# Batch 0 scores a tile whole in one step, tables first; all instruction orders set anew

## Chip, cores and metric

One NeuronCore of a Trainium2 chip runs one launch. The metric is device time in microseconds (us) of that core; times below are medians of whole launches, and the profile is one execution of the program.

## The reference, cut to what matters

Three layers run one after the other, in float32, on two batches (b = 0, 1) of 768 tokens and 512 channels (8 heads of 64).

```python
# 1. attention with a hash mask
q_bits = q @ proj > 0; k_bits = k @ proj > 0            # 6 bits each: a bucket of 64
scores = where(q_bucket == k_bucket, q @ k.T / 8, -1e9)
attn = exp(scores - max(scores)); attn /= sum(attn) + 1e-9
x = attn @ v                                            # heads side by side: 2 x 768 x 512
# 2. Fourier mixing and an MLP
u = x + real(fft2(x)); un = layernorm(u)
x = u + relu(un @ w_ch1) @ w_ch2                        # 512 -> 2048 -> 512
# 3. token mixing
theta = x @ w_theta
y = w_tok_r @ (x * cos(theta)) + w_tok_i @ (x * sin(theta))
u = x + y; out = u + relu(u @ w_ch)
```

The mask is computed as a product: a query has a one-hot vector of its bucket times a huge number, a key has its one-hot vector, and the product of the two is added to the scores in the same PSUM accumulator, so that a wrong bucket lies far below the maximum.

## The kernel before

All three layers are one program of 13,493 instructions on five engines, built in the order of a priority clock: `at(us)` sets the priority of what follows, `sooner(..)` moves it, and the table `T` holds some 300 such numbers. Batch 0's attention is different: `loop_ops` lists its steps with costs and buffers, `plan` orders them, and `attention_first` emits them in exactly that order (`Ordered.keep`). Priorities set an order when the program is built; on the chip each engine runs its own queue in that order and waits on semaphores.

The work in order of time:

- **Attention of batch 0**: four pairs of heads (`j`), per pair 12 tiles of 128 queries, head by head in turn; 48 tiles. Steps of a tile `n`: `S` (scores into a PSUM tile `pss` of two halves of 384 keys, a ring of three), `MAX` (VectorE), `EXP` (ScalarE), then either kind `d`: `HI` and `LO` split the weights into two float16 parts, `TR` transposes them by DMA; or kind `p`: `T` transposes on TensorE, `C` and `U` split. `AV` (18 small products) gives the output in `pso`, `N` normalises half a pair, `F` folds for the Fourier step.
- **How a score tile is made** (`phase_S`): a score half is a float32 product over the 64 dimensions of one head plus a bfloat16 product over 64 one-hot rows. Both use 64 of the 128 rows of TensorE, and the two row halves belong to the two heads. A step `S(n)` therefore does keys 384 to 767 of tile `n-1` and keys 0 to 383 of tile `n` (the other head) side by side, and `MAX(n)` needs `S(n+1)`.
- **Bits and patterns of a pair**: `load_pair` loads q and k transposed, `scale_pair` (GpSimd) scales k by 1/8, `bits_pair` does four products with `projb` and one comparison (`BP`, `BV`), `pattern_pair` does the one-hot vectors in four products with `pat` over 64 rows each (`PP`, `PA`).
- **Batch 1's attention** (`attention`, `prep`): scores there are float32r over stacks `stk` of 128 rows (high part, copy, low part, one-hot), four products a tile. `prep` loads (`tt`, `vr`), scales, makes bits, splits q and k and writes the one-hot rows. It runs beside the Fourier step of batch 0 (`Fft`, tables `ct`, `sn`, `dt` loaded on GpSimd's queue), the layer norm (`ln_first`, `layernorm`) and the MLP of batch 0 (`mlp1`, `mlp2`), whose weights are converted from an 8-byte form in pieces (`conv16`, `from_f64`: DMA `r`, two steps on ScalarE, one on VectorE, then a high and a low part).
- **Then** the Fourier step and MLP of batch 1, `theta`, `tok_sum` and `tok_out` of both batches, all on TensorE in dense order.

Products on data that nobody reads (`heat` before the first data, `fill` where batch 1 begins, 70 of them in `prep` and around the first tiles) fill stretches in which TensorE would have nothing to do. All of batch 0's instructions share line L64 and all others L62, since one helper records them; groups are told apart by tile names. Some tiles are borrowed: in batch 0 the names `w1h`, `w1l`, `p`, `pt` and `x` also stand for softmax tiles.

## Time and profile before

| | us |
|---|---|
| median of 3 launches | 710.55 (709.36 to 711.47) |
| the profiled execution | 712.29 |
| its span, first to last instruction | 710.5 |
| TensorE (PE) busy in the span | 663.8 (93%) |
| VectorE (DVE) | 415.6 (58%) |
| ScalarE (ACT) | 381.5 (54%) |
| GpSimd (POOL) | 313.7 (44%) |
| mean granted TensorE clock | 0.978 of full speed |

The profiled execution is 1.74 us above the median of the runs; 1.8 us of it lie outside the span. A busy share is a mean over stages with different limits: the stretches of time matter more than the totals here. SPq is the queue of SyncE, from which most DMAs start.

### The profile page before, as it was taken

The page shows a single profiled execution, that of the slowest core. Times are in us where ns is not written, and L with a number is a line of the kernel's source. Part 1 is how long each engine was busy: PE and PEld are TensorE (multiplying, and loading weights), DVE is VectorE, ACT ScalarE, POOL GpSimd, SP SyncE. Part 2 cuts the span into 40 slices and gives each one's busy share as a digit, 9 for nine tenths or more (in the row PEclk, how much of TensorE's full clock was granted, in tenths as well). Part 3 has the DMA queues.
Part 4 walks back from the last instruction along what each step waited for, and adds up shares of the span by engine and source line. Part 5 has one row for each costly group of instructions (what it writes and reads, how often), then busy time and mean ns, then how long its engine had stood idle before and what let it go on. Part 6 is the DMA issues. An engine that isn't in the chain of part 4 may idle for free.

```text
span 710.5 us, 13493 instructions
## 1 busy us (share of the span) xinstructions
PE 663.8 (93%) x5451; PEld 506.0 (71%) x5451; DVE 415.6 (58%) x687; ACT 381.5 (54%) x602; POOL 313.7 (44%) x257
## 2 busy tenths in 40 slices
PE   7899996896888889999999999999999999999998
PEld 2456664774675556866877687576685789999997
DVE  3668798869897568644494775452122676342222
ACT  4657887688788788463322176432026766720000
POOL 4678786576776566565020113421013457530000
PEclk9999999798899999999999999999999999999999
DMA  9987895596899997887450152100005723620202
GB/s 332 275 182 137 156 183 115 169 251 168 206 247 238 234 217 186 153 135 134 90 193 1 40 149 59 30 1 1 1 1 174 228 81 99 183 89 0 89 1 90
DMA packets 163038, 94.48 MB, mean 133 GB/s; under 512 B 138656, under 2 KB 149152, under 8 KB 162976
## 3 DMA queue, kind: packets, MB, share of 16 engines
q1 hardware_dynamic: 161040, 86.66, 52.1%
q0 software_dynamic: 1936, 6.96, 2.9%
q8 instruction: 43, 0.70, 0.4%
q14 instruction: 19, 0.16, 0.1%
HBM read 50.21 MB, written 6.29 MB: 80 GB/s over the span
## 4 chain that ended last, share of the span: by engine, by line
PE 26%; issue 11%; DMA 4%; POOL 3%; ACT 3%; DVE 3%; POOLq 0%; ACTq 0%; DVEq 0%; SPq 0%
PE psm L62 18%; PE psf L62 8%; DMA r<-in_wtok 3%; ACT r L62 1%; POOL w1l L62 1%; DMA x<-p 1%; POOL nn L62 1%; DVE u L62 1%; POOL wchl L62 1%; DMA r<-in_wch 1%; DVE rr L62 1%; ACT nn L62 0%; DVE xt L62 0%; POOL wthl L62 0%; ACT u L62 0%
## 5 line engine op out<-in xcount | busy, mean ns | idle before, releaser
L62 PE MATMUL psm<-unT,w1h 128*128 128x256 f16 x768 | 132.2, 276 | 2.5 <-DVE u L62 1.5
L62 PE MATMUL psm<-unT,w1l 128*128 128x256 f16 x384 | 106.0, 276 | 0.0
L62 PEld LDWEIGHTS <-w1h 128*128 128x128 f16 x768 | 75.3, 99 | 15.8 <-issue 3.4
L62 DVE SCALAR_TENSOR_TENSOR r<-r 128x512 uint32<-128x512 uint32 (+1 forms) x64 | 49.7, 779 | 52.5 <-ACT r L62 46.4
L62 PE MATMUL psm<-w2h,hl 128*128 128x512 f16 x192 | 73.2, 382 | 0.0
L62 PE MATMUL psm<-w2l,hh 128*128 128x512 f16 x192 | 72.9, 382 | 0.0
L62 PE MATMUL psm<-w2h,hh 128*128 128x512 f16 x192 | 72.3, 379 | 0.1
L62 POOL TENSOR_TENSOR w1l<-r,w1h 128x384 fp32r<-128x384 f32 (+1 forms) x33 | 36.9, 1129 | 76.6 <-ACT w1h L62 76.5
L62 ACT ACTIVATE r<-r,chalf 128x512 uint32<-128x512 uint32 (+1 forms) x64 | 46.0, 719 | 39.8 <-DMA r<-in_w 17.6
L62 PEld LDWEIGHTS <-hh 128*128 128x128 f16 x384 | 37.0, 98 | 42.5 <-issue 3.2
L62 ACT ACTIVATE hh<-psm 128x512 f16<-128x512 f32 x48 | 28.3, 592 | 65.7 <-PE psm L62 65.6
L62 DVE TENSOR_REDUCE nm<-pss 128x1 f32<-128x768 f32 x48 | 45.1, 949 | 21.0 <-PE pss L62 21.0
L64 PE MATMUL pss<-stk 64*128 64x384 f32 (+1 forms) x264 | 55.0, 482 | 0.8 <-ACT p L64 0.5
L64 DVE TENSOR_REDUCE nm<-pss 128x1 f32<-128x768 f32 x48 | 45.5, 954 | 16.1 <-PE pss L64 13.6
L62 DVE SCALAR_TENSOR_TENSOR hl<-psm,hh 128x512 f16<-128x512 f32 x48 | 32.9, 688 | 35.8 <-ACT hh L62 35.5
L62 PE MATMUL pss<-stk 128*128 128x384 f32 x192 | 47.9, 374 | 5.3 <-ACT p L62 4.7
L62 ACT ACTIVATE p<-pss,nm 128x768 f32<-128x768 f32 x43 | 38.4, 896 | 20.3 <-DVE nm L62 19.0
L62 POOL TENSOR_TENSOR p<-p,p 128x768 f16<-128x768 f32 x24 | 41.3, 1722 | 16.3 <-ACT p L62 10.6
L62 PEld LDWEIGHTS <-w1l 128*128 128x128 f16 x384 | 38.1, 99 | 6.0 <-issue 1.1
L62 PEld LDWEIGHTS pss<-stk 128*128 128x128 f32 x192 | 33.9, 199 | 10.2 <-ACT p L62 6.6
L62 ACT ACTIVATE r<-r 128x512 f32<-128x512 f32 (+1 forms) x64 | 39.4, 616 | 0.0
L62 PEld LDWEIGHTS <-hl 128*128 128x128 f16 x192 | 18.9, 98 | 21.2 <-issue 0.9
(333 smaller groups left out, 1572.2 us busy)
## 6 DMA issues: line engine op xcount, KB each, us to landing
r<-in_w SPq DMA_DIRECT2D x32, 512.0 KB, 4.7
r<-in_wtok SPq DMA_DIRECT2D x24, 384.0 KB, 3.6
vr<-in_v SPq DMA_DIRECT2D x8, 390.0 KB, 5.0
stk<-stk SPq DMA_DIRECT2D x16, 192.0 KB, 3.3
xT<-xs SPq DMA_DIRECT2D x12, 256.0 KB, 2.7
xt<-xT SPq DMA_DIRECT2D x4, 768.0 KB, 5.2
ct<-in_ct POOLq DMA_DIRECT2D x4, 579.0 KB, 7.2
sn<-in_sn POOLq DMA_DIRECT2D x4, 576.0 KB, 9.1
```

Source lines behind the costliest of these rows:

```text
L62: return fn(*a, **k)
L64: self.last = fn(*a, **k)
```

## The change

The table `T` is set anew throughout: costs (`du`), keys (`lk`), the kinds of the 48 tiles (`kq`, still 32 `d` and 16 `p`), engines (`hq`, and new `lq`, `pk`) and nearly all offsets. Two switches in it: `sf='rrrr'` leaves all four pairs of batch 1 in the form they had (float32r stacks of 128 rows; the new branch `whole` in `prep` is built for none), and `mt=0` lets `mlp2` run two token tiles in turns, in two PSUM tiles at once. In code:

```diff
-    projb = mk(const, [128, 32], F32, "projb")
+    small = mk(at_p, [128, 290], F32, "small")
+    proj, hb = small[:, 0:96].rearrange("p (a n) -> p a n", a=3), small[:, 96:98]
+    pats = mk(at_p, [128, 6, 128], BF16, "pats")
...
     def load_pair(j, n):
+            made[j] = [t[:, 0:2], two3(t[:, 2]), two3(t[:, 3].bitcast(BF16)), hk]
+        if n < 2:
+            SY.dma_start(out=made[j][0][:, n], in_=A["qd"][0, j, :, n])
+        else:
+            SY.dma_start(out=made[j][1] if j else raw, in_=A["kd"][0, j])
...
+    def bit_products(ps, q, k, h):
+        for g in range(2):
+            mm(ps[64 * h + 32 * g:64 * h + 32 * g + 32], proj[:, 0], q[:, h, 384 * g:384 * g + 384], True, g == 1)
+        mm(ps[64 * h:64 * h + 32], proj[:, 1], k[:, h], False, True)
...
     def pattern_pair(j, n, ps, by="v"):
+        if j:
+            mm(ps, pats[:, 3 * h + p], bits[j], True, True)
+        else:
+            mm(ps, pat[half[h], p], bits[j][half[h]], True, True)
...
-    def phase_S(n, ps):
-        for g, m in ((1, n - 1), (0, n)):
+    def halves_S(ps, ops, c, part=(0, 1)):
+        for k in part:
+            for g in range(2):
+                mm(ps[:, g, 0:384], ops[2 * k][half[g], c], ops[2 * k + 1][half[g]], k == 0, k == 1)
...
-            op(("MAX", n), "DVE", 0.87, n + 1, [("S", n + 1)])
+            op(("MAX", n), "DVE", 0.87, n + 1, [("S", n)])
-                op(("LO", n), "POOL", 1.7, n + 4, [("HI", n)], "", [("p", ("EXP", n))])
+                op(("LO", n), *(("DVE", 0.97) if T["lq"][n] == "v" else ("POOL", T["dl"])), n + 4, [("HI", n)], "", [("p", ("EXP", n))])
...
+                pt[n], turned = transposed(p2.pop(n))
+                for g, k in (("d1", 0), ("dw", 1)):
+                    if n >= T["cn"][k] and g not in gate:
+                        gate[g] = turned
...
-        with sooner("cl"):
+        with sooner("cl"), after_gate("dw"):
...
+            with after_gate("d1"):
+                ld.dma_start(out=o, in_=i[b, j])
```

In the diff, `small` holds `proj`, `hb` and the pattern tables in one load; `qd` is q of one head on both row halves, `kd` has keys 0 to 383 on the lower and 384 to 767 on the upper half; `T` has `cn=[31, 27]`. The two gates mean that the loads of batch 1's first q and k (`tt`) and of the first MLP weights (`r`) are issued only behind the transposes of batch 0's tiles from 31 and 27 on; nothing held them before. Counts by engine: five `LO` steps go from GpSimd to VectorE, two `HI` steps from ScalarE to GpSimd; a pair has six products for its bits (was four) and six for its patterns (was four), the results of the latter read by ScalarE (18) and VectorE (6), where it was ScalarE 13 times and VectorE once; three low parts of weights go from GpSimd and one high part from ScalarE to VectorE. The matrix products of the scores, `AV` and of all later layers are the same in number and shape. Runs of score products in batch 0 that stand between other work are 37, where 43 were.

The order as built, at three places. First SyncE's queue at the start (names `in_..` are inputs in HBM: `qT`, `kT`, `qd`, `kd` queries and keys, `w` MLP weights). Before:

```order
L64 DMA stk<-in_qT 128x768
L64 DMA stk<-in_kT 128x768
L62 DMA tt<-in_qT 128x768
L62 DMA tt<-in_kT 128x768
L62 DMA r_1895<-in_w 128x1024
L62 DMA r_1902<-in_w 128x1024
L62 DMA r_1909<-in_w 128x1024
L64 DMA vr<-in_v 128x780
L64 DMA stk<-in_qT 128x768
L64 DMA_TRANSPOSE w1h<-p_112 128x12x128 x2
```

and now:

```order
L64 DMA ident<-in_ident 128x128
L64 DMA pats<-in_pats 128x768
L64 DMA pat<-in_patr 128x256
L64 DMA stk<-in_qd 128x768 x2
L64 DMA stk<-in_kd 128x768
L64 DMA_TRANSPOSE pt<-p_112 128x12x128
L64 DMA vr<-in_v 128x780
L64 DMA_TRANSPOSE w1h<-p_112 128x12x128
```

The five loads of `tt` and `r` no longer stand ahead of the first transposes.

Second, TensorE at its first data (`zero` and, before, `w1h` are operands of `heat`; `x`, `w1l` are borrowed tiles of one-hot keys and raw keys). Before:

```order
L64 MATMUL pss<-stk,projb 32x384 x4
L64 LDWEIGHTS w1h
L64 MATMUL psm<-w1h 128x512
L64 LDWEIGHTS w1h
L64 MATMUL psm<-w1h 128x512
L64 LDWEIGHTS pat
L64 MATMUL pss<-bits,pat 128x384
```

and now:

```order
L64 MATMUL pso<-stk,small 32x384 x2
L64 MATMUL pso<-w1l,small 32x384
L64 MATMUL pss<-stk 128x384 x2
L64 LDWEIGHTS small
L64 MATMUL psm<-bits,small 128x384
L64 LDWEIGHTS small
L64 MATMUL pss<-bits,small 128x384
L64 MATMUL pso<-stk,small 32x384 x2
L64 MATMUL pso<-w1l,small 32x384
L64 LDWEIGHTS stk
L64 MATMUL pss<-x,stk 128x384
```

The first head's bits come alone, its first scores stand between bits and patterns, and the two `heat` products behind the bits are gone.

Third, VectorE where batch 0 ends and batch 1 begins (`psm<-pso,r` is the last normalisation, which frees `pso`; `vv<-vr,vv` is the low part of batch 1's values). Before:

```order
L62 TENSOR_SCALAR bits<-pss 64x768
L62 SCALAR_TENSOR_TENSOR stk<-tt,stk 64x768
L64 TENSOR_SCALAR r<-pso 128x6
L62 SCALAR_TENSOR_TENSOR vv<-vr,vv 128x780
L64 RECIPROCAL r<-r 128x6
L64 TENSOR_TENSOR psm<-pso,r 128x384
L62 TENSOR_TENSOR fa<-x,psm 128x6x64 x2
```

and now:

```order
L62 TENSOR_SCALAR bits<-pss 64x768
L62 SCALAR_TENSOR_TENSOR stk<-tt,stk 64x768
L64 TENSOR_TENSOR hlz_194<-zraw,hlz_194 128x6x64
L64 TENSOR_SCALAR r<-pso 128x6
L64 RECIPROCAL r<-r 128x6
L64 TENSOR_TENSOR psm<-pso,r 128x384
L62 SCALAR_TENSOR_TENSOR vv<-vr,vv 128x780
```

The values' step now follows the normalisation. On TensorE at this place 70 `fill` products stood ahead of batch 1's first two score tiles; now 50 stand ahead of the first tile and 20 more ahead of the next two. The first product of the batch 0 MLP stood behind 59 score tiles (11 of batch 1) and 54 `AV` steps, and stands behind 61 and 54.

## Rows read from the trace of the kernel before

**Rows 1.** The page: busy tenths in 40 equal slices, TensorE and its granted clock.

```profile
PE   7899996896888889999999999999999999999998
...
PEclk9999999798899999999999999999999999999999
```

**Rows 2.** Stretches: length, busy us (instructions) by engine, clock, DMA share, GB/s.

```profile
core 0: us, PE busy (x) PEld busy (x) DVE busy (x) ACT busy (x) POOL busy (x), PEclk, DMA share, GB/s
9.00:37.00 28.00, 23.81 (x181) 12.97 (x181) 18.22 (x21) 18.83 (x27) 18.50 (x19) 0.94 1.11 313
...
77.00:118.00 41.00, 40.27 (x594) 27.30 (x592) 35.19 (x57) 32.66 (x50) 30.43 (x22) 1.00 0.88 151
118.00:136.00 18.00, 9.58 (x98) 8.55 (x95) 16.64 (x26) 15.96 (x24) 9.27 (x6) 0.81 0.43 111
...
160.00:190.00 30.00, 20.47 (x154) 15.93 (x151) 27.77 (x59) 24.63 (x37) 19.65 (x15) 0.78 0.80 206
190.00:240.00 50.00, 45.52 (x464) 33.28 (x462) 39.50 (x64) 41.33 (x62) 36.37 (x24) 1.00 1.03 220
240.00:282.00 42.00, 35.21 (x308) 23.88 (x306) 28.90 (x39) 34.89 (x51) 25.88 (x18) 0.96 0.92 223
...
355.00:550.00 195.00, 194.74 (x1289) 137.67 (x1286) 94.72 (x200) 72.34 (x129) 39.51 (x44) 1.00 0.20 58
```

**Rows 3.** Timeline at the start: start, length, instruction, [idle before it, releaser].

```profile
6.01 1.51 PE L64 MATMUL pss<-stk,projb 128*32 128x384 f32 x8 [1.65 <-DMA projb<-in_projb]
...
7.57 0.56 DVE L64 TENSOR_SCALAR bits<-pss 128x384 bf16<-128x384 f32 x1 [6.39 <-PE pss L64]
...
11.51 1.82 DVE L64 TENSOR_REDUCE nm<-pss 128x1 f32<-128x768 f32 x2 [1.22 <-PE pss L64]
```

**Rows 4.** Timeline, 16 to 31 us: SyncE's queue, GpSimd, the first AV.

```profile
16.04 11.38 SPq L64 DMA_TRANSPOSE w1h<-p  x2
...
29.66 0.83 POOL L64 TENSOR_SCALAR p<-p 128x768 f16<-128x768 f32 x1 [2.91 <-DMA w1h<-p]
...
30.16 0.73 PE L64 MATMUL pso<-vv,w1h 128*128 128x65 f16 x18
```

**Rows 5.** Timeline of TensorE inside batch 0: bits, scores, a pattern product.

```profile
44.35 0.85 PE L64 MATMUL pss<-stk,projb 128*32 128x384 f32 x8
...
54.86 1.89 PE L64 MATMUL pss<-stk 64*128 64x384 f32 x12
...
57.90 0.33 PE L64 MATMUL psm<-bits,pat 64*128 64x384 bf16 x1
57.90 1.15 PE L64 MATMUL pss<-stk 64*128 64x384 f32 x6
...
89.27 1.08 PE L64 MATMUL pss<-stk 64*128 64x384 f32 x6
```

**Rows 6.** Timeline where batch 1 begins: VectorE, ScalarE, TensorE.

```profile
118.97 2.59 DVE L62 SCALAR_TENSOR_TENSOR stk<-tt,stk 64x768 fp32r<-64x768 f32 x1
...
121.68 2.40 DVE L62 SCALAR_TENSOR_TENSOR vv<-vr,vv 128x780 f16<-128x780 f32 x1
...
124.92 3.64 ACT L62 ACTIVATE stk<-pss,hb 64x768 fp32r<-64x768 f32 x4
...
124.83 6.03 PE L62 MATMUL pso<-pat 128*128 128x120 bf16 x70 [5.03 <-DVE psm L64]
...
135.21 2.75 PE L62 MATMUL psm<-sn,hlz 128*128 128x384 f32 x9 [2.87 <-DVE psm L62]
```

**Rows 7.** Timeline of TensorE around the layer norm of batch 0.

```profile
168.01 0.79 PE L62 MATMUL pss<-bits,pat 64*128 64x384 bf16 x2 [3.66 <-ACT p L62]
...
184.75 0.61 PE L62 MATMUL psm<-unT,w1h 128*128 128x256 f16 x2 [1.48 <-DVE u L62]
```

**Rows 8.** Groups of instructions: busy us, mean ns; low parts on VectorE and GpSimd.

```profile
L62 DVE SCALAR_TENSOR_TENSOR p<-p,p 128x768 f16<-128x768 f32 x4 | 4.0, 1010 | 0.5 <-ACT p L62 0.3 <-POOL p L62 0.2
...
L64 POOL TENSOR_TENSOR p<-p,p 128x768 f16<-128x768 f32 x7 | 11.8, 1688 | 2.8 <-ACT p L64 2.7
```

More of the change, by code (lines that the diff above doesn't have):

```diff
@@ L240, in fused_kernel, with load_pair @@
     bits, stk = {}, []
[L242 removed]
+    def load_pair(j, n):
+        if not stk:
+            stk.extend(mk(st_p, [128, 4, S], F32, "stk") for _ in range(2))
         if j not in made:
[L245 to L250 removed]
@@ new lines, in bits_pair, with see, pattern_pair @@
+        q, k = made[j][0], made[j][1] if j else raw
+        def see(r):
+            V.tensor_scalar(out=bits[j][r], in0=ps[r], scalar1=0.0, scalar2=None, op0=ALU.is_gt)
+        if not j:
+            return [lambda h=h: (bit_products(ps, q, k, h), see(half[h])) for h in range(2)]
+        for h in range(2):
+            bit_products(ps, q, k, h)
+        return lambda: see(slice(0, 128))
+    HOT = (("k", 0), ("q", 0, 0), ("k", 1), ("q", 1, 0), ("q", 0, 1), ("q", 1, 1))
+    def pattern_pair(j, n, ps, by="v"):
+        qk, h = HOT[n][:2]
+        g = HOT[n][-1]
+        p = 2 if qk == "k" else g
+        if j:
+            mm(ps, pats[:, 3 * h + p], bits[j], True, True)
+        else:
+            mm(ps, pat[half[h], p], bits[j][half[h]], True, True)
+        if qk == "q":
+            out = made[j][2][:, h, 384 * g:384 * g + 384]
+            return lambda: AC.activation(out=out, in_=ps, func=AF.Relu, bias=hb[:, 0:1])
+        out = made[j][3][:, h]
+        if by == "v":
@@ L437, in attention @@
                 at(t0 + pace * n - lead)
-                with after_gate("p1" if b else None):
-                    run(prep(b, j))
+                new = prep(b, j)
+                for k in range(5):
+                    at(t0 - lead + T["p0"][k])
+                    with after_gate(None if not k else f"e{k}" if f"e{k}" in gate else "p1"):
+                        next(new)
             st, vv = made[i]
@@ L474, in attention @@
                             new = prep(b, j + 1)
+                            next(new)
                         next(new)
@@ L498, in start @@
                 return None
-            return max([at_[o["eng"]]] + [ends[d] + (0 if d in own else lag[ops[d]["eng"]]) for d in wait])
+            change = T["ws"] if o["eng"] == "PE" and (n[0] == "S") != split[0] else 0
+            return change + max([at_[o["eng"]]] + [ends[d] + (0 if d in own else lag[ops[d]["eng"]]) for d in wait])
+        split = [True]
         order = []
@@ L573, in loop_ops, with attention_first @@
         return ops
-    def attention_first(pace, after, start):
+    def attention_first(pace, after, start, ps, nm):
         x_t[0] = mk(x_p, [128, NT, DM], F32, "x")
         N = 8 * NT
-        p, p2, pt, o, ps, nm, then, values, folds, low = ({} for _ in range(10))
+        p, p2, pt, o, then, values, folds, low, last = ({} for _ in range(9))
         kind = lambda n: T["kq"][n]
@@ L654, in attention_first @@
             emit(*op)
-            if op == ("MAX", 1):
-                run(start)
+            if op == ("EXP", 1):
+                next(start)
+            if op == ("MAX", 3):
+                next(start)
             if op == ("EXP", N - 1):
@@ L1080, in fused_kernel @@
     SY.dma_start(out=ident, in_=A["ident"])
+    SY.dma_start(out=pats, in_=A["pats"].bitcast(BF16))
     heat(T["wm"])
     see = bits_pair(0)
-    heat(T["wn"])
-    scale_pair(0)
-    see()
-    one_hot = [pattern_pair(0, n, (0, 1), "s") for n in range(2)]
-    for do in one_hot:
-        do()
-    next(values)
+    see[0]()
+    scale_pair(0, slice(0, 1))
+    scale_pair(0, slice(1, 2))
+    wide = PS("s")
+    first = {n: PS("s") for n in range(2)}
+    phase_S(0, first, (0,))
+    heat(T["wn"])
+    pattern_pair(0, 0, PS("m")[:, 0:384])()
+    pattern_pair(0, 1, wide[:, 0, 0:384])()
+    see[1]()
+    phase_S(0, first, (1,))
+    tops = {0: attn_max(first[0])[0]}
+    phase_S(1, first, (0,))
+    pattern_pair(0, 2, PS("m")[:, 0:384])()
+    pattern_pair(0, 3, PS("o")[:, 0:384])()
+    if "r" in T["sf"]:
+        SY.dma_start(out=patr, in_=A["patr"].bitcast(BF16))
     Ordered.keep = False
```

316 lines of the change are left out of this document (181 added, 135 removed).

## The prediction, made blind

> **What bounds the kernel now.** I read the page's strip of forty slices first. TensorE is at 9 almost throughout from about 280 us, with ragged digits before that and two dips near 125 and 165 us; its clock falls in the same places [rows 1]. The stretches put numbers on it: from 355 to 550 us TensorE is busy 194.74 of 195 us at full clock, so nothing can be won there by order. Before 282 us it idles: 4.2 us between 9 and 37, only 0.7 between 77 and 118, then 8.4 (118 to 136), 9.5 (160 to 190), 4.5 (190 to 240) and 6.8 (240 to 282) [rows 2]. The lower clock costs (1 - clock) times the length: 1.7, 3.4 and 6.6 us in three of these. So whatever brings the dense part forward shortens the kernel, and whatever only speeds up an engine beside it does not. The two stretches with most idle time are also those where VectorE is fullest: 16.6 of 18 us and 27.8 of 30 us [rows 2].
>
> The sum is made against the profiled execution, 712.29 us, which is 1.74 us above the median of the runs.
>
> **The change, part by part.**
>
> *First tile sooner.* Before, the bits of both heads are one group of products from 6.01 us on, the comparison comes at 7.57, and the first maximum at 11.51, since both score halves of two tiles, and both one-hot vectors at full width, stand before it [rows 3]. Now one head goes first: the loads it needs are 145 KB larger, some 0.5 us at 313 GB/s [rows 2]; three of the bits' products instead of four, 0.85 x 3/4 = 0.64 us [rows 5], end near 7.2; comparison 0.56 [rows 3] and hand-overs, 7.9; pattern 0.33 [rows 5] and its reading, about 0.6, 8.9; the second score half, under half of 1.08 [rows 5], and the maximum starts near 9.4. That is 2.1 us sooner. I take -2.0, with 0 as the other end if the larger load lands last.
>
> *Transposes no longer behind the bulk loads.* The first two transposes hold SyncE's queue for 11.38 us from 16.04 on; GpSimd then waits 2.91 us at 29.66 for one of them to give back its buffer, and the first AV starts at 30.16 [rows 4]. Ahead of them stood 5.1 MB of loads, by their shapes; now 3.2 MB do. 1.9 MB at 313 GB/s [rows 2] is 6 us. TensorE can get back no more than what it lost in this stretch, 4.2 us of idle and 1.7 of clock, 5.9 together. I take -3.5, between 0 and -5.9, since VectorE (18.2 of 28) and ScalarE were not free in it either.
>
> *More products for bits and patterns.* Six for four at the bits: 0.85 x 2/4 = 0.42 us for each of three pairs, +1.3. Patterns: a 64-row product now slides in beside the scores: with it the score step beside it takes 1.15 instead of 1.08, so 0.07 is its cheapest price and its own 0.33 the dearest [rows 5]. With 128 rows it can't lie beside 64-row work. Six at 0.25 less four at 0.12 is 1.0 a pair, +3.0 at most and 0 at least; I take +1.7. Together +3.0.
>
> The Trainium skill (TensorEngine Tiling (Array Packing), Key Properties) says that changing the tiling mode drains TensorE, while tiles of one mode run side by side, which speaks against exactly this part. The trace agrees as far as the step with a pattern beside it goes, 1.15 against 1.08 us [rows 5]; by the rule alone all 18 patterns would sit at the dear end, and the sum would be 1.3 us worse.
>
> *Whole tiles.* The products of a tile are the same: two halves side by side on the two row halves, now of one tile. Nothing is won per tile. Two tiles back to back take 1.89 us, one alone 1.08 [rows 5], so standing together saves 0.13 each; six runs fewer give -0.8, and a few AV runs that merge as well -0.3: -1.1. That the maximum no longer waits for the next tile's step shortens the loop through three PSUM tiles; from 77 to 118 us TensorE is busy 40.27 of 41 [rows 2], so there this changes nothing and I count it inside the early term.
>
> *Five low parts on VectorE.* GpSimd takes 1.69 us for one, VectorE 1.01 [rows 8], but another product of two SBUF operands on VectorE took 2.40 us beside GpSimd's subtractions [rows 6]. VectorE has 35.2 of 41 us in the dense stretch [rows 2]. I take 0, hidden behind TensorE; were that cover gone, 5 to 12 us, carried as a rival below.
>
> The Trainium skill (SBUF — State Buffer, Who interferes with whom) has the reason for such a spread: a VectorE instruction with two SBUF inputs contends with a GpSimd instruction that reads SBUF, and one blocks for the whole of the other. The 2.40 us against 1.01 agree [rows 6, 8].
>
> Batch 0 in sum: -2.0 - 3.5 + 3.0 - 1.1 = -3.6.
>
> *Where batch 1 begins.* TensorE idles 5.03 us until the last normalisation has freed `pso`, then does 70 fills in 6.03 us, and only then the first scores [rows 6]. VectorE was late with the normalisation because 2.40 us of batch 1's values stood before it; that step is now behind it, and 20 fills fewer stand before the first score: 20 x 6.03/70 = 1.7. So the first scores come 2.4 + 1.7 = 4.1 us sooner, just when the first two one-hot rows of ScalarE's four are there (124.92 + 1.8 = 126.7; the new start is 130.7 - 4.1 = 126.6). But the Fourier products wait at 135.21 for VectorE [rows 6], whose work up to there is the same. I take -2.5 between -4.1 and 0: one or two score tiles move forward into idle time.
>
> *To the MLP.* Three maxima more (0.91 each, [rows 3]) stand on VectorE before the first MLP result is read, one more low part (1.0 to 2.4) and some ten steps on two columns, which I bound by that stretch's mean step, 27.77/59 = 0.47 [rows 2]: 4 to 9 us, 5.5 taken. Part of it fills the holes in which TensorE waited 3.66 us for an exponential [rows 7]. Between +5.5 (all late) and -8 (half of the stretch's 9.5 idle and 6.6 clock, [rows 2]) I take -1.0.
>
> *Two token tiles at once in the second MLP product* hold two of three PSUM tiles, so a first-product chunk between them may wait for its eviction, some 1.3 us, twice at most: 0 to +2.6, taken +0.6. Batch 1's scores keep their form: nothing.
>
> Sum: -3.6 - 2.5 - 1.0 + 0.6 = -6.5. 712.29 - 6.5 = 705.8 profiled; less 1.74, **704.0** for the median. From 282 us on there is little room for a gain to be lost again, since TensorE there waits for nothing.
>
> **The rivals.**
>
> *The middle closes too* (about 694.6): with scores further ahead, the stretch from 160 to 282 us gives back half of its 20.8 us of idle. For it: the waits there are single exponentials and transposes, not one engine's sum. Against it: VectorE has 27.8 of 30 us in the worst of it [rows 2]. That is -10.4 in the place of -1.0, so 9.4 less than 704.0: 694.6.
>
> *The lead is eaten* (about 710): from 118 to 136 us VectorE is the limit, 16.6 of 18 [rows 2]; if it, not the fills, decides when the Fourier step starts, and batch 0 ends only as much sooner as its extra products allow, the two ends of the early terms leave -1: 709.5 to 711.
>
> *VectorE becomes the bound, slower* (about 714.5): five low parts at 0.97 to 2.4 us, pattern reading on VectorE (six at 0.56 less one at 1.0: +2.3), and 5.5 us more before the MLP. At 2.4 each that is 12 + 2.3 + 5.5 = 19.8. VectorE's free time is 5.8 us in the dense stretch and 3.6 in the two tight ones [rows 2], 9.4 in all, and 10.4 us would lie on the path: against the 6.5 won elsewhere, +3.9, or 714.5. It decides from the point where a low part costs over about 1.5 us on average, each of them holding the maxima queued behind it, and with them the exponential and the PSUM tile TensorE waits for. For it: 2.40 in rows 6; against it: 1.01 in rows 8, and GpSimd is relieved by the same five steps.
>
> *How the numbers follow.* My forecast 0.46 (699 to 708.4), middle closes 0.24, lead eaten 0.12, VectorE slower 0.18. A change under 0.3% (2.1 us: 708.4 to 712.7) is about what a measurement of this kernel can't tell from none. Faster by more 0.70, within it 0.12, slower by more 0.18. The likeliest gives 704.0; the range for eight in ten leaves out the outer half of the slow rival and the far end of the fast one: 691 to 714.
>
> **What would show it.** Right: the first maximum near 9.4 us; the first AV before 26 us and no wait of GpSimd for a transpose before it; the first scores of batch 1 some 7 us sooner than 130.7; pattern products at 0.25 to 0.33 us of their own; the dense part from about 282 us on unchanged in length and 6 to 7 us earlier. Wrong: VectorE over 90% between 37 and 118 us with low parts above 1.5 us each; the first MLP product not earlier than 184.75 [rows 7], or new waits of TensorE for its buffers beyond 282 us.

## The result, and the profile after

The kernel after takes 713.57 us (median of 18 launches, 708.98 to 718.72), the kernel before 710.93 us on the same chip (18 launches); the ratio is 1.0051, with a 95% interval of 1.0028 to 1.0073. The change makes the kernel 2.6 us slower, where 704.0 us was forecast. One launch of e11 below took over 1.5% more than the fastest of its kernel and is left out of every figure (with it e11's median is 715.29). The profiled execution of after took 712.62 us (span 710.9, mean clock .974), only 0.3 us more than that of before: the traces compare two executions that differ by less than the medians do.

| us, profiled executions | before | after | shift |
|---|---|---|---|
| first maximum starts | 11.51 | 10.02 | -1.5 |
| first `AV` starts | 30.16 | 27.09 | -3.1 |
| last `AV` of batch 0 ends | 118.53 | 114.68 | -3.85 |
| first scores of batch 1 | 130.67 | 123.93 | -6.7 |
| Fourier step of batch 0 goes on without a break from | 135.21 | 135.25 | 0 |
| first product of batch 0's MLP | 184.75 | 188.27 | +3.5 |
| Fourier step of batch 1, products with `dt` | 388.9 | 385.4 | -3.5 |
| last layer, products with `wchh` | 656.6 | 656.6 | 0 |

So the early gain came, was lost twice (before 135 us, and from there to 188 us), half of it came back, and it was lost again before the last layer. (Landmarks of the same kernel differ from one execution to the next: in the traces of the runs below the first maximum of the new batch 0 starts at 9.8 to 12.9 us; and since the order of the work behind batch 0 differs, the last two say where a piece of work stands, not how much is done by then.)

The page's strip of after, which answers to [rows 1], is better in the first six slices only (8 9 9 9 9 9 for 7 8 9 9 9 9). Both dips are still there (6 and 8 became 7 and 7, 6 and 8 became 5 and 7), and the clock row beneath is no better than it was.

```profile
PE   8999997795787999999999999999999899999997
...
PEclk9999998898699999999999999999999999999999
```

The stretches of after answer to [rows 2]; 550 to 600 us is new.

```profile
core 0: us, PE busy (x) PEld busy (x) DVE busy (x) ACT busy (x) POOL busy (x), PEclk, DMA share, GB/s
9.00:37.00 28.00, 25.56 (x231) 13.08 (x230) 23.25 (x30) 20.89 (x32) 20.46 (x19) 1.00 1.12 309
...
77.00:118.00 41.00, 36.23 (x586) 25.19 (x585) 37.23 (x57) 29.45 (x45) 28.65 (x21) 1.00 0.96 194
118.00:136.00 18.00, 11.83 (x91) 11.03 (x91) 17.55 (x30) 14.86 (x22) 10.52 (x7) 0.69 0.61 164
...
160.00:190.00 30.00, 18.54 (x116) 15.19 (x116) 24.51 (x49) 25.29 (x37) 23.92 (x17) 0.71 0.78 197
190.00:240.00 50.00, 42.40 (x443) 31.93 (x442) 39.35 (x71) 38.05 (x58) 29.18 (x22) 0.97 1.01 219
240.00:282.00 42.00, 38.78 (x377) 26.19 (x376) 29.37 (x42) 34.44 (x51) 21.61 (x15) 1.00 1.02 230
...
355.00:550.00 195.00, 193.50 (x1264) 136.14 (x1263) 94.71 (x196) 74.81 (x133) 39.53 (x43) 1.00 0.22 58
550.00:600.00 50.00, 47.65 (x247) 41.24 (x245) 27.89 (x44) 31.60 (x57) 22.93 (x24) 0.97 0.36 117
```

The same stretch of before, for the last of them:

```profile
550.00:600.00 50.00, 48.42 (x255) 42.27 (x254) 34.13 (x49) 35.09 (x65) 28.24 (x28) 1.00 0.43 129
```

Two columns are to be read together: what TensorE leaves idle, and (1 - clock) times the length. From 9 to 37 us both got better (idle 4.2 to 2.4 us, clock .94 to 1.00). From 118 to 136 us the idle time fell from 8.4 to 6.2, but the clock from .81 to .69: 3.4 us at the lower clock became 5.6. From 160 to 190 us idle rose from 9.5 to 11.5 and the clock's part from 6.6 to 8.7; from 190 to 282 us idle is about as it was (11.3 and 10.8). From 550 to 600 us, where the forecast saw no room for a loss, idle rose by 0.8 and the clock's part by 1.5. From 77 to 118 us VectorE has become the fuller engine, 37.2 of 41 us against TensorE's 36.2, and TensorE's idle time rose from 0.7 to 4.8 us: 2.3 of it before the last `AV` of batch 0 ends at 114.68, the rest behind it.

**Where the waits are now.** The longest waits of TensorE from 100 to 282 us, before and then after (what waited, what for; total us, times, longest):

```profile
PE pss L62 <- ACT p L62: 10.1, 8, 3.7
PE pso L62 <- DVE psm L64: 5.0, 1, 5.0
```

```profile
PE pss L62 <- ACT stk L62: 5.3, 2, 4.8
PE pss L62 <- ACT p L62: 5.1, 3, 2.3
PE psm L62 <- DVE unT L64: 4.9, 1, 4.9
PE pso L62 <- DVE psm L64: 3.2, 1, 3.2
```

Eight waits for exponentials, the longest of 3.7 us, became three; two single waits of 4.8 and 4.9 us stand in the list that before does not have. The timeline of after shows both (start, length, instruction, [idle before it, releaser]):

```profile
161.69 0.75 ACT L62 ACTIVATE r<-r,chalf 128x512 uint32<-128x512 uint32 x1 [2.94 <-DMA r<-in_w]
...
163.02 1.80 ACT L62 ACTIVATE stk<-pss,small 64x768 fp32r<-64x768 f32 x2
...
164.88 1.65 PE L62 MATMUL pss<-stk 128*128 128x384 f32 x4 [4.80 <-ACT stk L62]
...
181.51 3.43 PE L62 MATMUL psm<-dt,fa 128*128 128x128 f32 x15 [4.86 <-DVE unT L64]
...
188.27 0.61 PE L62 MATMUL psm<-unT,w1h 128*128 128x256 f16 x2 [0.37 <-DVE u L62]
```

At the first, ScalarE stood 2.94 us at the conversion of a weight piece whose load had not landed, with the one-hot rows of the next scores queued behind it. At the second, TensorE waited for VectorE to write the low part of the transposed normalised tile. What the clock does around them, in stretches of 5 us of after:

```profile
160.00:165.00 5.00, 0.20 (x2) 0.13 (x1) 3.06 (x6) 3.25 (x5) 3.39 (x3) 0.72 0.96 238
165.00:170.00 5.00, 5.00 (x47) 4.38 (x48) 2.64 (x6) 5.00 (x8) 2.42 (x2) 0.60 0.51 129
...
180.00:185.00 5.00, 3.49 (x17) 3.52 (x17) 4.71 (x5) 4.95 (x7) 3.80 (x3) 0.50 0.55 144
185.00:190.00 5.00, 4.63 (x18) 2.89 (x18) 4.38 (x11) 4.70 (x8) 4.92 (x4) 0.50 0.83 223
```

After each long wait TensorE is busy again but at 0.60 and 0.50 of its clock, that is, at 1.2 GHz for much or all of the stretch: the fifteen products with `dt` behind the second wait take 3.43 us, and 1.90 us where the same fifteen run at full clock (172.81 us).

**The same over all launches.** Each launch has its span and its mean granted clock, so the span can be split into what the clock takes, span x (1 - mean clock), and the rest. In before the first is 13.7 to 14.2 us and the rest 693.9 to 695.2 (means of the sets of launches beside the experiments). In after they are 20.6 and 691.3. By this split the change saves about 3 us of work and waits, and gives 6.6 us to the clock. Among after's own launches the mean clock goes with the time, from .978 at 708.98 us to .964 at 718.72; in some other kernels (e5, e8) the two hardly go together. Over the 99 launches of before beside the experiments a straight line through time against clock's part has a slope of 0.4, so that a microsecond in the clock's part goes with 0.4 us of time there. This split is an account, not yet a cause: an idle engine at the lower clock loses nothing, and a wait at half clock counts half in either part.

For the two traced executions the idle time can be taken out. With busy time x (1 - clock) summed over stretches of 1 us, an estimate, the lower clock costs TensorE 11.9 us in before and 14.7 in after, 2.8 more, where the split has 15.6 and 18.5. Its idle time is 46.7 and 45.3 us (span less busy time), 1.4 less. So in this pair the clock's loss is larger than what the idle time gave back, but it is less than half of 6.6. The experiments test it.

### The profile page after: what moved, and what is told of

Its sections match the earlier page's. It is cut to its first block, busy times and chain, and to the rows that moved or that the text cites. A ratio compares the mean times of both kernels' runs of the same rounds, so it can differ in the third digit from the quotient of the medians.

```text
span 710.9 us, 13554 instructions
## 1 busy us (share of the span) xinstructions
PE 665.6 (94%) x5473; PEld 507.9 (71%) x5473; DVE 423.2 (60%) x702; ACT 382.2 (54%) x606; POOL 299.6 (42%) x250
## 5 line engine op out<-in xcount | busy, mean ns | idle before, releaser
L62 PEld LDWEIGHTS <-w1h 128*128 128x128 f16 x768 | 74.8, 99 | 20.6 <-issue 8.9
L62 DVE SCALAR_TENSOR_TENSOR r<-r 128x512 uint32<-128x512 uint32 (+1 forms) x64 | 54.4, 853 | 45.6 <-ACT r L62 42.4
L62 PE MATMUL psm<-w2l,hh 128*128 128x512 f16 x192 | 60.8, 379 | 0.2 <-DVE w2l L62 0.2
L62 PE MATMUL psm<-w2h,hl 128*128 128x512 f16 x192 | 60.8, 380 | 0.0
L62 PE MATMUL psm<-w2h,hh 128*128 128x512 f16 x192 | 60.1, 379 | 0.5 <-ACT w2h L62 0.5
L62 PE MATMUL pss<-stk 128*128 128x384 f32 x192 | 49.4, 381 | 9.0 <-ACT stk L62 5.3
L62 POOL TENSOR_TENSOR w1l<-r,w1h 128x384 fp32r<-128x384 f32 (+1 forms) x32 | 38.5, 1219 | 31.4 <-ACT w1h L62 31.2
L62 POOL TENSOR_TENSOR p<-p,p 128x768 f16<-128x768 f32 x23 | 38.7, 1686 | 17.0 <-ACT p L62 10.6
L64 PE MATMUL pss<-stk 64*128 64x384 f32 x192 | 42.6, 520 | 1.3 <-ACT p L64 1.1
L62 PEld LDWEIGHTS pss<-stk 128*128 128x128 f32 x192 | 34.3, 202 | 12.9 <-ACT stk L62 5.8
```

The source lines that it names most:

```text
L62: return fn(*a, **k)
L64: self.last = fn(*a, **k)
```

## The experiments

Every kernel is set against launches of before on the same chip; after stands first. The sets ran on several chips, with medians of before from 709.23 to 711.05 us, so kernels of different sets are best compared by their ratios. There are 18 launches of after and 5 to 12 of every other kernel.

| kernel | median us | ratio to before (95%) | clock's part | rest |
|---|---|---|---|---|
| after | 713.57 | 1.0051 (1.0028 to 1.0073) | 20.6 | 691.3 |
| e1 new batch 0, numbers behind it as before | 723.33 | 1.0207 (1.0178 to 1.0236) | 23.6 | 698.7 |
| e2 old batch 0, numbers behind it as after | 723.63 | 1.0199 (1.0175 to 1.0224) | 22.8 | 698.8 |
| e3 one token tile at a time | 716.02 | 1.0094 (1.0064 to 1.0125) | 18.9 | 695.6 |
| e4 low parts on GpSimd | 731.64 | 1.0316 (1.0287 to 1.0345) | 28.0 | 702.0 |
| e5 new batch 0, rows behind it as before | 711.53 | 1.0015 (0.9994 to 1.0035) | 14.0 | 695.5 |
| e6 old batch 0, rows behind it as after | 715.77 | 1.0075 (1.0048 to 1.0102) | 19.4 | 694.2 |
| e7 low parts on GpSimd, rows held | 718.30 | 1.0125 (1.0089 to 1.0161) | 20.8 | 696.1 |
| e8 two waits moved | 713.79 | 1.0046 (1.0025 to 1.0068) | 21.1 | 690.8 |
| e9 fills in three waits | 711.11 | 1.0010 (0.9988 to 1.0032) | 15.1 | 694.3 |
| e10 both of these | 712.42 | 1.0030 (1.0002 to 1.0059) | 16.6 | 694.3 |
| e11 before with fills | 714.27 | 1.0044 (1.0008 to 1.0080) | 10.6 | 701.5 |
| e12 longer fills | 712.79 | 1.0047 (1.0022 to 1.0073) | 14.4 | 697.3 |
| e13 patterns over 64 rows | 711.09 | 1.0019 (0.9997 to 1.0041) | 19.5 | 690.2 |
| e14 loads not held back | 717.64 | 1.0117 (1.0081 to 1.0154) | 20.7 | 695.7 |
| e15 e13 and e9 together | 711.09 | 0.9993 (0.9966 to 1.0020) | 13.9 | 695.0 |

### e1, e2: each half of the change with the other half's numbers

`T` was split: the numbers of batch 0 from one kernel, those of all that follows from the other. In e1 (e2 is its mirror image):

```diff
-        f0=60.74, w1=75.66, w1s=2.14, b1=124.07, pace1=2.0, w2=142.1, w2s=0.42, m0=194.62, f1=227.68, th=206.87, m1=282.69, z0=309.76,
...
+        f0=87.52,
+        w1=91.45,
+        w1s=0.57,
+        b1=124.69,
```

> Batch 0 as changed, everything behind it (all times and offsets of batch 1's attention, of the weight conversions, of both MLPs and of the token mixing) as in the kernel before. Theory 1, the new order behind batch 0 loses what batch 0 won: the last AV of batch 0 ends near 114.7 us as in the changed kernel (118.5 before), the first MLP product comes a few us before 184.75 and the time is 711 - 3.8 = about 707 (705 to 709), some 6 below the changed kernel. Rival, the lead is eaten whatever the order, because VectorE and the chain to the first normalisation set the time there: the first MLP product stays at 184 to 186 and the time is 710 to 712. Rival 2, the new form of batch 0 costs something behind it (later loads): 713 or more.

> The other half alone: batch 0 as in the kernel before, all times and offsets behind it as in the changed kernel. Theory 1 (the new order loses): the order costs what the whole change costs plus what batch 0 won, 711 + 2.6 + 3.8 = about 717 (715 to 719), with the first MLP product at 190 or later. Rival, order neutral and the lead eaten anyway: 710 to 713.

Both came out at 723 us, worse than either parent and outside every number expected of them but e1's "713 or more", so this was no test of the halves. One wait shows why, in e1's view of waits from 355 to 550 us and in its timeline of SyncE's queue:

```profile
PE psm L62 <- DMA unT<-u: 9.1, 1, 9.1
...
406.91 0.34 SPq L62 DMA_DIRECT2D r<-in_wth  x1
408.16 0.33 SPq L62 DMA_DIRECT2D r<-in_wtok  x1
408.71 1.25 SPq L62 DMA_TRANSPOSE unT<-u  x1
```

The second transposed tile of batch 1's `u` is queued behind two weight loads, and TensorE stands for 9.1 us at 400 us, in the stretch in which it is idle for 0.3 us in all in before [rows 2]. In e2 the same wait is 8.3 us. The scheduler orders by a simulated timeline: a number changed in batch 0 moves instructions everywhere behind it. Neither set of numbers served with the other's batch 0.

### e3: token tiles one after the other

```diff
-        e2='pppppppvppvvvvvv', sl='vpppppppvpvpvpvp', mt=0, uc='apaaaa',
+        mt=1,
```

> The changed kernel, but the second MLP product takes one token tile at a time again. The prediction gave the pair +0.6, so 713.6 - 0.6 = about 713. Rival, the pair holds two of three PSUM tiles and that is where the time from 190 us on is lost: 3 us or more faster, about 710. If the pair saves something: 714 to 715.

716.0 us, 2.5 above after: undoing the turns won nothing. What the turns cost or gain stays open, since this edit too moved the order elsewhere.

### e4, e7: the low parts back on GpSimd

```diff
-        lq='pvpppppvpppvvpppvpppvpvppvpvvppppppvvpppppvvpppp',
+        lq='pppppppppppppppppppppppppppppppppppppppppppppppp',
```

> The changed kernel, but the five low parts of batch 0 that VectorE does are back on GpSimd. Prediction: they cost nothing on VectorE, and GpSimd gets 5 x 1.7 = 8 us more in a stretch where it has time, so the time stays at 713.6 within 1, batch 0 ending within 1 us of 114.7. Rival (VectorE is the bound and these low parts hold its maxima): batch 0 ends 2 or more us sooner and the time is 2 to 4 us lower, 710 to 711.5.

731.6 us, but with the wait of e1 and e2 again (10.0 us), so e7 repeats it with the order held. This is the way of all kernels from e5 on: at the end of the program each engine's instructions behind the attention of batch 0 are tied in a row by order alone, taken from one of the two kernels; batch 0 has its own order from `plan` as ever. (Five VectorE steps at the Fourier step of batch 0 stand a few places otherwise than in after, in all kernels held to its rows. e8 has that too, and its time is that of after.)

```diff
+    for e, codes in ROWS.items():
+        row, ahead = (unpack(c) for c in codes)
...
+            if k:
+                tc.add_manual_dep(mine[x], mine[row[k - 1]].name, edge, reason="row")
```

> The changed kernel with the five low parts of batch 0 on GpSimd (as e4), but everything behind batch 0 held in the changed kernel's rows, so that only batch 0 differs. e4's trace has batch 0's last AV end 1.6 us later (116.3), so by the rows alone 1.6 us at most are lost: 713.6 + 0 to 1.6. Rival (the low parts themselves carry the 18 us of e4): over 720.

718.3 us: 4.7 more than after, nearly all of it outside the clock's part (691.3 to 696.1). The five low parts on VectorE are a gain, and a larger one than the 0 to 1.6 us expected. From 77 to 118 us VectorE falls from 37.23 to 33.65 us busy without TensorE getting more done (36.18 us), and the last `AV` ends at 115.29, 0.6 later than in after. How 0.6 us there becomes 4.7 at the end was not traced.

### e5, e6: the two halves with rows held

> Batch 0 as changed; everything traced behind it stands, engine by engine, in exactly the row in which the kernel before issues it (edges of issue order, no waits added), so that, unlike in e1, nothing else is shuffled. Theory 1 (batch 0 really wins 3.8 us and the new rows behind it lose them): the lead at the last AV, 114.7 against 118.5, is carried through unchanged rows, and the time is 711 - 3.8 = about 707, at most 709. Rival (the lead is eaten by VectorE between 115 and 135 us whatever the rows): first MLP product at 184 to 185 as before, and 710 to 712.

> The other half: batch 0 as before, everything behind it in exactly the rows of the changed kernel. Theory 1: the new rows cost what the change costs and what batch 0 won, 711 + 2.6 + 3.8 = about 717 (715 to 719). Rival (rows neutral, lead eaten anyway): 711 to 714, as the changed kernel itself.

With before's rows behind it, the new batch 0 gives 711.5: within the measurement, equal to before. With after's rows the old batch 0 gives 715.8. So the loss goes with the new order behind batch 0 (clearly with the old batch 0 ahead of it, likely with the new one, where the intervals of e5 and after overlap), and it shows in the clock's part: 14.0 us with before's rows, whichever batch 0 stands ahead, and 19.4 and 20.6 with after's. Only the pair of new batch 0 and new rows turns the lead into a smaller rest: 691.3 against 694.2 to 695.5 in the other three. e6 also holds the first loads of batch 1 and of the weights back, as after does; its batch 0 ends at 121.7 in the trace, later than in before or after.

Over its launches e5 makes nothing of the lead, but its trace shows that the lead can pass the Fourier step under the old order. There the products start here, beside 135.21 in before [rows 6]:

```profile
131.44 3.13 PE L62 MATMUL psm<-sn,hlz 128*128 128x384 f32 x9 [3.68 <-DVE hle L62]
```

The first MLP product follows at 181.5 and the last layer at 652.7, some 3 and 4 us sooner than in before. The traced launch took 708.68 us, next to the fastest of its twelve; where the median launch loses the lead is not shown.

### e8: the two long waits taken apart

On ScalarE the one-hot pair was put ahead of the conversion that waits for its load; the `unT` steps went ahead of conversions there, and on VectorE ahead of a maximum, a conversion and part of the residual `u`. ScalarE's order at the first place, as the difference to after:

```order
 L62 ACTIVATE w1h<-r_1993 128x512
+L62 ACTIVATE stk<-pss,small 64x768 x2
 L62 ACTIVATE r_2000<-r_2000,chalf 128x512
 L62 ACTIVATE r_2000<-r_2000 128x512
-L62 ACTIVATE stk<-pss,small 64x768 x2
```

> The changed kernel with its own rows, but two places moved: on ScalarE the two one-hot steps of batch 1's second head (stk<-pss at 163.0) go ahead of the weight conversion that waits 2.9 us for its load, and the first normalised transposes (unT) go ahead of a weight conversion on ScalarE and of a maximum and the next residual sums on VectorE. Theory (the middle is lost at in-order queues, where a late load or a slow conversion stands ahead of what TensorE waits for): the waits of 4.8 us at 164.9 and 4.9 us at 181.5 shrink to under 2 each, the first MLP product comes 3 to 6 us sooner than 188.3, and 2 to 5 us are left at the end: 709 to 711.5. Rival (VectorE is full there, the time only moves): 713 to 714.

713.8 us and the same clock. The view of waits from 100 to 282 us shows the waits moved, not removed:

```profile
PE pss L62 <- ACT p L62: 12.3, 7, 3.8
PE pss L62 <- ACT stk L62: 4.4, 2, 3.8
```

The wait for `unT` is gone from the head of the list, and waits for exponentials came back for it. The wait for `stk` stayed: ahead of the pair ScalarE now stands 4.79 us at another step of the conversions, which waits for VectorE. From 160 to 190 us ScalarE and VectorE are busy 25.3 and 24.5 of 30 us in after; that what is put forward there delays what it passes is likely, not traced step by step.

### e9, e10, e11, e12: products without use in the waits

Products on data that nobody reads, 35, 55 and 55 of them, were put where after waits for `hlz`, for `stk` and for `unT`. If lower clock after the waits is what costs, this should win it back.

```diff
+                    fill({0: 35, 4: 55}.get(n, 0))
...
+            heat_in(live["o"][:, 392:512], 55)
```

> The changed kernel in its own rows, with dummy products (as the kernel's own fills, 128x120) added where TensorE stands in the three long waits: 35 before the Fourier products, 55 before the first score step behind the one-hot wait (164.9), 55 behind the score step ahead of the unT wait (181.5). Over 18 runs of the changed kernel the mean granted clock is 0.971, over 33 of the kernel before 0.980: span x (1 - clock) is 20.6 against 13.9 us, while span x clock is 691.3 against 694.3. Theory 2 (the change wins 3 us of work and waits and loses 6.7 at a lower TensorE clock, because its longer waits stand close together): the fills hold the clock up from 160 to 193, mean clock 0.977 to 0.98, and 4 to 6 us come back: 707.5 to 709.5. Rival (the clock isn't the loss; fills only take TensorE's time): 713.6 to 716 with clock below 0.973.

> e8 (two waits moved) with the same fills as e9. e8 had the lowest span x clock so far, 690.8, with clock 0.970. Theory 2: clock back to 0.977 to 0.98, 707 to 709. Rival: 713 to 716.

> The kernel before in its own rows with fills in its own three waits (35 before the Fourier products at 135.2, 45 ahead of the pattern products at 168.0, 25 at 182.3). What fills give the kernel before: theory 2 says its clock loss is 14 us with some 6.6 of them between 160 and 190, so a few of these come back there too: 706 to 709. Rival (the clock can't be held by fills): 710 to 713.

711.1 us, 2.5 less than after, between the theory's number and the rival's. The clock's part fell by 5.5 us (20.6 to 15.1) and the rest rose by 3.0, some of which only changes sides in the split, as a wait filled at full clock no longer counts half in each. Without the idle time, in the trace: the clock's loss over busy time fell from 14.7 to 10.7 us and the idle time from 45.3 to 39.2, while some 8 us of fills came in (145 at 3.06/55 each). The timeline and the stretch of e9:

```profile
159.24 3.06 PE L62 MATMUL pso<-small 128*128 128x120 bf16 x55
...
164.47 1.41 PE L62 MATMUL pss<-stk 128*128 128x384 f32 x4 [2.17 <-ACT stk L62]
...
160.00:190.00 30.00, 24.00 (x227) 20.36 (x225) 28.38 (x57) 26.67 (x39) 22.29 (x16) 0.83 0.74 191
```

The clock from 160 to 190 us rose from .71 to .83, and the first MLP product came at 186.7 in place of 188.3; between the fills' end and the next data there are still 2.2 us. With the moves of e8 as well (e10) it is no better. In before (e11, with 35, 45 and 25) fills lower the clock's part from 14.2 to 10.6 and raise the rest by 7: slower. So these fills did not win back what before loses to the clock; 714.3 us is above both numbers that were expected.

The longer fills of e12 (40, this time ahead of batch 1's scores, then 80 and 85) were to tell whether more of the clock can be had:

```diff
-                    fill({0: 35, 4: 55}.get(n, 0))
+                    fill({0: 40, 4: 80}.get(n, 0))
...
-            heat_in(live["o"][:, 392:512], 55)
+            heat_in(live["o"][:, 392:512], 85)
```

> e9 with the fills made as long as the waits: 40 ahead of the score step at 130.5 (in e9 35 stood behind it, at half clock, and held the Fourier products up), 80 in the wait before 164.5, 85 in the one before 180.9. In e9 the clock loss fell from 20.6 to 15.1 us and span x clock rose by 3.0, because TensorE still fell to half clock behind both waits (164.5 to 168.7, 180.9 to 188.6). Theory 2: with the waits covered these two low stretches go, clock 0.983 or more, and the time falls below both kernels: 705 to 709. Rival (fills take from the products behind them what the clock gives): 711 to 714 with a higher clock.

They did not help: against e9 the clock's part fell by another 0.7 us and the rest rose by 3.0. Fills run in the same queue as the work; where in the span they take back what they give was not traced.

### e13: patterns over 64 rows

```diff
-        if j:
-            mm(ps, pats[:, 3 * h + p], bits[j], True, True)
-        else:
-            mm(ps, pat[half[h], p], bits[j][half[h]], True, True)
+        mm(ps, pat[half[h], p], bits[j][half[h]], True, True)
```

> The changed kernel, but batch 0's pattern products are over 64 rows again, all else in the same rows. The prediction's term: 128 rows cost 0 to 3.0 us, 1.7 taken, so batch 0's last AV would end near 113.0 instead of 114.7, and the time 0 to 1.7 lower, 712 to 713.6. Rival (no price: they stand alone either way): last AV at 114.7 and 713.6 within 1.

711.1 us, 2.5 less by the medians and 1.1 less in the rest: the 18 products over 128 rows cost 1 to 2.5 us. The intervals of the two ratios, 1.0028 to 1.0073 and 0.9997 to 1.0041, overlap, so the sign is likely and the size is not sharp. In e13's trace the last `AV` ends at 113.23, near the 113.0 expected, but in e12's, whose patterns are over 128 rows, it ends at 113.04, so this landmark does not settle it.

### e14: loads not held back

```diff
-        with sooner("cl"), after_gate("dw"):
+        with sooner("cl"):
...
-            with after_gate("d1"):
+            with nullcontext():
```

In the rows the loads of batch 1's q and k and of the first weights were put back ahead of the first transposes.

> The changed kernel, but the first three weight loads and the first two loads of batch 1 (2.3 MB) go ahead of the first transpose again, as before, all else in the same rows. The prediction's term: the transposes gained 3.5 us (0 to 5.9) by not standing behind them; so the first AV comes some 3 us later than 27.1, at 30, batch 0 ends 2 to 3.5 us later, near 117.5, and, as e5 and e6 showed a batch-0 lead of 3.8 to be worth 0 to 3 at the end, 713.6 + 0 to 3. Rival (the loads were not what held the first transposes): first AV at 27 to 28, time unchanged.

717.6 us, 4.1 above after, all of it outside the clock's part. SyncE's queue in e14 (its start, and what answers to [rows 4]):

```profile
16.98 6.82 SPq L64 DMA_DIRECT2D vr<-in_v  x1
23.89 5.72 SPq L64 DMA_TRANSPOSE w1h<-p  x1
```

In after the same transpose ends at 21.81, here at 29.61, and the first `AV` starts at 30.2 in place of 27.09, as expected. Batch 0 ends at 121.2 in this trace, later than the 117.5 expected; the traced launch is the slowest of e14's six (723.37).

### e15: the two edits that helped, together

e13's products with e9's fills.

> The kernel after with two of the earlier edits together: batch 0's pattern products over 64 rows, and 35, 55 and 55 products without use in three of TensorE's longer waits; all other rows as after. Theory (the loss is batch 0's wider products, about 2.5 us, and lower clock behind them, of which fills win back about 2.4 net): the two add, 713.6 - 2.5 - 2.5 = 708.6, with a mean clock of .978 to .980 and a clock loss of 14 to 16 us; that would be below the kernel before. Rival (both edits only shift the same slack, since each alone ends at 711.1): 710.5 to 711.5, no sum.

711.09 us beside 711.05 for before in the same set; 0.9993 (0.9966 to 1.0020). The rival's number: the fills lowered the clock's part by 5.6 us again, and the rest rose by 4.8 of them. It is the best version of the study by its ratio, but it can't be told from before. The two losses do not simply add up; how much of either is left in it stays open.

## Why the prediction was wrong, point by point

**The terms of batch 0 held in sum.** The first maximum came 1.5 us sooner (taken: 2.0). The start of SyncE's queue and the first `AV`, beside [rows 3, 4]:

```profile
10.02 0.96 DVE L64 TENSOR_REDUCE nm<-pss 128x1 f32<-128x768 f32 x1
...
14.71 3.30 SPq L64 DMA_TRANSPOSE pt<-p  x1
...
18.94 2.87 SPq L64 DMA_TRANSPOSE w1h<-p  x1
...
27.09 0.72 PE L64 MATMUL pso<-vv,pt 128*128 128x65 f16 x18
```

The first transposes take 3.3 and 2.9 us instead of 11.4 for two, GpSimd no longer waits for one, and the first `AV` is 3.1 us sooner (forecast: over 4). Undone alone, this part cost 4.1 us (e14), above the 0 to 3 expected there; -3.5 was about the right size. In e6, the old batch 0 with the same loads held back, the first two transposes take 7.2 us together, which agrees. The wider bits and patterns and the low parts, beside [rows 5, 8]:

```profile
38.90 1.81 PE L64 MATMUL pss<-stk,small 128*32 128x384 f32 x12
...
40.07 1.43 DVE L64 SCALAR_TENSOR_TENSOR p<-pt,p 128x768 f16<-128x768 f32 x1
...
42.94 0.34 PE L64 MATMUL psm<-bits,pats 128*128 128x384 bf16 x1
```

Twelve products for bits take 1.81 us (1.50 in the next pair) where eight took 0.85: 0.65 to 0.96 a pair, not the 0.42 that was scaled from their number. A pattern product has 0.32 to 0.34 of its own, the dear end of the forecast. (That end was summed too low: six at 0.33 less four at 0.07 is 1.7 a pair, 5.1 in all, not 3.0.) The Trainium skill (TensorEngine Tiling (Array Packing), Key Properties) says that a change of tiling mode drains TensorE; e13, which keeps these products in the mode of the scores, agrees in sign with 1 to 2.5 us for 18 of them. Batch 0 ended 3.85 us sooner; -3.6 was forecast. That the sum came so near is in part luck, with single terms off by up to a microsecond and the gain of whole tiles not measured alone.

**VectorE did not become the bound in the way of that rival.** Its time, 714.5, is nearest to the result, but not for its reason: the five low parts took 0.95, 1.43, 0.95, 0.95 and 1.44 us, 1.14 on average, below the 1.5 from which it was to decide, and moving them back costs 4.7 us (e7). VectorE is 91% busy from 77 to 118 us, but 88% over the whole of 37 to 118, for which the sign of being wrong was named, and the lead of batch 0 came all the same.

**First step that failed: where batch 1 begins, -2.5.** The first scores came 6.7 us sooner, as forecast. But the timeline at this place, beside [rows 6], shows what the Fourier step made of it:

```profile
118.39 0.57 DVE L64 TENSOR_TENSOR psm<-pso,r 128x384 f32<-128x384 f32 x1
...
119.01 5.16 PE L62 MATMUL pso<-small 128*128 128x120 bf16 x50 [3.16 <-DVE psm L64]
...
123.93 1.27 PE L62 MATMUL pss<-stk 128*128 128x384 f32 x4
...
133.16 1.01 PE L62 MATMUL psm<-ct,hle 128*128 128x386 f32 x2 [2.86 <-DVE hlz L62]
...
135.25 2.13 PE L62 MATMUL psm<-ct,hlz 128*128 128x386 f32 x6
```

Two of its products start at 133.16, after 2.86 us of waiting for VectorE, and the others at 135.25. VectorE is busy 17.55 of 18 us there. Of the forecast one part came: four score tiles stand ahead of 135.25, two more than before, and TensorE's idle time from 118 to 136 us fell by 2.2 us, of which the clock took as much (3.4 to 5.6). But the lead of batch 0 itself did not pass: up to here the sum had it at 6.1 us, and the step goes on where it did before. The prediction noted that the Fourier products wait for VectorE "whose work up to there is the same", and still let the lead pass. The work is not the same. Two low parts of values now stand on VectorE between the last normalisation and the first Fourier product:

```profile
118.87 1.69 DVE L62 SCALAR_TENSOR_TENSOR vv<-vr,vv 128x780 f16<-128x780 f32 x1
...
130.37 1.14 DVE L62 SCALAR_TENSOR_TENSOR vv<-vr,vv 128x780 f16<-128x780 f32 x1
```

In before the first stood ahead of the normalisation (121.68, [rows 6]) and the second began at 135.06, as the Fourier data was ready. From the end of the normalisation to that point VectorE took 10.4 us in before and 14.2 here, and these two make 2.8 of the difference. A lead eaten by VectorE was one of the rivals, put at 0.12; the row for it was on the table (16.6 of 18 in [rows 2]). e5, where the old order stands behind the same batch 0, fed the step at 131.44: so it is this order of VectorE's work, not a full VectorE alone, that ate the lead. Earlier score tiles in front of a step that another engine feeds are work moved, not all of it time won.

**Second step that failed: to the MLP, -1.0.** The first MLP product came 3.5 us later than before, where the sum up to there had it 7.1 sooner. The term's own range (+5.5 to -8) took half of the idle time and of the lower clock as something that could be won back; it was costed by VectorE's extra steps. The step came out at +3.5, inside that range and far from the -1.0 taken. What happened was neither: from 160 to 190 us fewer waits stood, two of them longer than any there before (4.8 and 4.9 against 3.7), idle time rose by 1.9 us and the clock's part by 2.1, while VectorE was busy for less (24.5 us against 27.8).

**What had no term: the clock.** The prediction read off that the lower clock costs 1.7, 3.4 and 6.6 us in three stretches, and then had the clock only as something that might be won back, with no term for a loss. In the launches it is the largest change of all, 6.6 us of the split against 3 us of gain elsewhere; over busy time alone the traced pair shows 2.8. e5 and e6 place it in the rows behind batch 0 (14.0 us with the old, 19.4 and 20.6 with the new). e9 makes it likely that it is a cause and not only an account: products of no use in three waits took 5.5 us out of the clock's part and 2.5 us off the time (the intervals of e9 and after overlap). It is not settled: longer fills gave less (e12), the same fills gave nothing clear of the noise beside e13 (e15), and in before they cost time (e11). The Trainium skill (TensorE: Matmul & The Clock Gate, What's actually happening) says that the throttled state is the default and that activity of the array releases it. The trace agrees: 0.50 in the stretches behind the 4.86 us wait, and .83 in place of .71 from 160 to 190 us once the waits are filled. That the merging of short waits into long ones is what lowered the clock is read from the rows alone: e8, which was to undo it, moved the waits and left the clock as it was. Why the new order runs at a lower clock stays open.

**"From 282 us on there is little room for a gain to be lost"** held in after for most of it: the Fourier step of batch 1 stands 3.5 us earlier than before. It is gone by the last layer. The two kernels' products by tile, before and then after (count: fastest/mean/slowest ns, first and last start):

```profile
L62 PE MATMUL psf<-u,wchh x64: 334/334/341, 656.6 to 706.5; 128*128 128x384 f32 x64
L62 PE MATMUL psf<-dt,fa x54: 220/276/412, 388.9 to 404.1; 128*128 128x128 f32 x27, 128*128 128x256 f32 x18, 128*1 128x128 f32 x6, 128*1 128x256 f32 x3
```

```profile
L62 PE MATMUL psf<-u,wchh x64: 332/334/346, 656.6 to 706.7; 128*128 128x384 f32 x64
L62 PE MATMUL psf<-dt,fa x54: 220/276/410, 385.4 to 400.7; 128*128 128x128 f32 x27, 128*128 128x256 f32 x18, 128*1 128x128 f32 x6, 128*1 128x256 f32 x3
```

One new wait of 2.4 us, for a converted piece of the token weights, and the clock of .97 behind it stand between (550 to 600 us), and 1.2 us more idle before (355 to 550). And e1, e2 and e4 show how deep that part can fall: 8 to 10 us on a single transfer. That a stretch has no idle time does not mean that no transfer in it can be late.

**Two token tiles at once** (+0.6): no run shows their price; e3 was slower, not faster, but with the order moved elsewhere too.

## What to carry to other kernels

Read the mean granted clock with the span, and give the clock a term of its own: here a schedule with less idle time of TensorE, but two longer waits, ran at a lower clock and was slower, though that the longer waits are the reason was not shown. Where the clock is charged over a whole span, take the idle time out. Follow a lead to the step that another engine feeds, read that engine's order up to there, and count the lead only as far as that engine is sooner too. Under a scheduler that orders by a simulated timeline, test one part of a change with the order of all the rest held, or the test measures the new order.

## What the runs showed of the hardware

The mean granted clock of one and the same kernel on one core differs from launch to launch (.964 to .978 in after); over those launches the time differs by 9.7 us and goes with the clock, which it hardly does in e5 and e8. In after TensorE ran at 1.2 GHz for all of 180 to 190 us, 8.1 of these 10 us busy. And filling waits on purpose gave little: in e9 and e12 (against after) and e15 (against e13) the clock's part fell by 5.5, 6.2 and 5.6 us, and the rest rose by 3.0, 6.0 and 4.8; in e11, against before, the two are 3.6 and 7.
